# Left-over query tiles, 128-token blocks and a tighter pipeline in the first two batches of a fused attention and feed-forward kernel

## The chip, the cores and the metric

The kernel runs on one core of a Trainium2 chip. The metric is the device time of one execution in microseconds (us). The core has a matrix engine (TensorE, PE in the profile), whose weight loads are listed apart (PEld), a vector engine (VectorE, DVE), a scalar engine (ScalarE, ACT), a general engine (GpSimd, POOL) and a sync engine (SyncE, SP) that here only starts DMAs. Each engine has its own queue of instructions, and the kernel writes their order out by hand.

## The reference

Inputs are q, k and v of shape 8 x 8 x 576 x 64 (batches, heads, positions, head size) in float32, and the weights w_in (512 x 2048) and w_out (2048 x 512) in float64, which the kernel converts to float32 itself. What is computed:

```python
scores = scale * np.matmul(q, k.transpose(0, 1, 3, 2))
kth = np.partition(scores, -32, axis=-1)[..., -32:-31]
scores = np.where(scores >= kth, scores, -1000000000.0)
attn = np.exp(scores - np.max(scores, axis=-1, keepdims=True))
attn = attn / (np.sum(attn, axis=-1, keepdims=True) + 1e-09)
x = np.matmul(attn, v)        # -> tokens x 512
h = x @ w_in
out = (h * np.clip(h + 3.0, 0.0, 6.0) / 6.0) @ w_out
```

In words: attention in which each query keeps its 32 largest scores, and after it a feed-forward layer with a hard-swish between its two matrix products.

## The kernel before

**Tiles.** The 576 positions of a head are split into four tiles of 128 queries (qt 0 to 3) and 64 left-over queries (qt 4). Two heads make a Pair; two Pairs make a Duo, the unit of work. A batch has eight full duos (four tiles by two halves of the heads) and two left-over duos, ten in all, 80 in the kernel. In batches 0 to 6 a left-over duo stands after the two duos of tile 0 and another after those of tile 2; in batch 7 both stand after tile 0.

**Slots.** A duo is eight slots (loop `for i in range(8)`). In each slot `top` (L249, L253) makes one of four rounds that find the next eight largest of a row and strike them out: slots 0 to 3 for the first Pair, 4 to 7 for the second. A full duo has two rows per Pair and round, a left-over duo one. The scores of the next duo (L226, L229; L214, L216 for left-over ones) are issued in slot 1, in duo 0 in slot 3; ScalarE copies them from PSUM (L232, L235).

**Parts.** What follows the maxima is queued at fixed distances, in slots from the duo's start, separately for its two Pairs (tables `usual`, `early` for the first two duos and `soon` for the last two): `shift` (GpSimd, L262, L265), `exp` (ScalarE: two activations a row and the sum, L272, L277, L282), `inverse` (VectorE reciprocal, L286), `weights` (GpSimd: a multiply, L296, and a copy that splits words into 16-bit halves, L305), `flip` (a transposing DMA on SP, L311), `join` (puts the halves together, L317: ScalarE for the first Pair, GpSimd for the second) and `values` (the product with v on TensorE, L337, and ScalarE's copy to xT or xr, L344). In a full duo of the table `usual`, exp is at 4 and 8, values at 20.

**Feed-forward pieces.** When the values of a tile are complete, a block is put in the list `todo`: 128 tokens (16 pieces) in batches 0 and 7, 256 tokens (32 pieces) in batches 1 to 6, and 128 left-over rows of two batches together (xr, one buffer). A piece is 16 of the trace's matmuls of the first product (L361; 8 in a block of 256 tokens) or 4 of the second (L383). ScalarE takes the first product out of PSUM (L369, L371), GpSimd gates it (L375, L376). Per duo 6 to 9 pieces are issued (3 to 5 in a left-over duo), more when more are waiting (`left`). Before a new xT is begun, the pieces of the last block but one are all issued (`blocks[-2]`).

**Weight chunks.** w_in and w_out come in 32 chunks of 512 columns, one per slot. `convert` starts a DMA (L102); in a later slot ScalarE takes the absolute value (L108) and the low words (L111) and GpSimd clamps (L109); VectorE shifts and merges (L117, L118) and GpSimd adds (L122). With two chunks under way VectorE's and the add of the older are issued two slots after its clamp. All chunks are converted within the first four duos.

Of the kernel before, what the change touches and what calls it, by code (L numbers as in the profile page):

```python
# [29 lines left out]
def kernel(  # L30
# [9 lines left out]
    nc = tc.nc  # L40
    P = nc.NUM_PARTITIONS
    B, H, S, D = q.shape
    DM, FF = moe_w_in.shape
    J = S // P
# [51 lines left out]
    def convert(dst, src):  # L96

        st = kqpool.tile([P, 2 * WC], U32, tag="kq", name="st")
        nc.sync.dma_start(st[:], src)  # L102
        yield
        words = st[:].rearrange("p (n two) -> p n two", two=2)
        lo, hi = words[:, :, 0], words[:, :, 1]
        a = gpool.tile([P, WC], F32, tag="g", name="a")
        y = gpool.tile([P, WC], F32, tag="g", name="y")
        nc.scalar.activation(a[:], hi.bitcast(F32), AF.Abs)  # L108
        nc.gpsimd.tensor_scalar(a[:], a[:], HI_MOST, HI_LEAST, ALU.min, ALU.max)  # L109

        nc.scalar.activation(y[:], lo, AF.Copy, bias=2.0, scale=2.0**-51)  # L111
        yield

        au, yu = a[:].bitcast(U32), y[:].bitcast(U32)
        nc.vector.tensor_scalar(au, au, 3, None, ALU.logical_shift_left)  # L117
        nc.vector.scalar_tensor_tensor(  # L118
            out=yu, in0=hi, scalar=0x80000000, in1=yu,
            op0=ALU.bitwise_and, op1=ALU.bitwise_or,  # L120
        )
        nc.gpsimd.tensor_tensor(  # L122
            dst.bitcast(I32), a[:].bitcast(I32), y[:].bitcast(I32), ALU.add
        )
# [13 lines left out]
    class Pair:  # L138


        def __init__(self, b, hp):
            self.b, self.hp = b, hp
            self.vm, self.vr, self.kr = vms[hp], vrs[hp], krs[b % 2 * NHP + hp]
# [40 lines left out]
    class Duo:  # L184
# [4 lines left out]


        def __init__(self, pairs, qt):
            self.pairs, self.qt = pairs, qt
            self.rest = qt == J
            self.nt = 1 if self.rest else 2
            self.nb = J + 2 if self.rest else 2 * J + 1
            self.m, self.less = [None] * 2, [None] * 2
            self.e16, self.t16, self.eT = [None] * 2, [None] * 2, [None] * 2
# [115 lines left out]
        def join(self, u):  # L313

            eT = self.eT[u] = kqpool.tile([P, 2 * J + 1, P], F32, tag="kq", name="eT")
            copy = nc.gpsimd.tensor_copy if u else nc.scalar.copy
            copy(  # L317
                eT[:, 0 : self.nb, :]
                .rearrange("p c q -> p (c q)")
                .bitcast(U16)  # L320
                .rearrange("p (x h) -> p h x", h=2),
                self.t16[u][:, 0 : 2 * self.nb, :].rearrange("p (h c) q -> p h (c q)", h=2),
            )
# [77 lines left out]
    pairs = [[Pair(b, hp) for hp in range(NHP)] for b in range(B)]  # L401
    duos = []
    for b in range(B):
        halves = [pairs[b][0:2], pairs[b][2:4]]
        for qt in range(J):
            duos += [Duo(h, qt) for h in halves]

            if b == B - 1 and qt == 0:
                duos += [Duo(h, J) for h in halves]
            elif b < B - 1 and qt % 2 == 0:  # L410
                duos.append(Duo(halves[qt // 2], J))
    assert J == NHP == 4
    per_batch = 2 * J + 2
    ND = len(duos)
    todo = []
    blocks = []
    left = 0
# [2 lines left out]
    def piece(count=1):  # L420
        nonlocal left
        for _ in range(count):
            while todo:
                try:
                    gates.append(next(todo[0]))
                    left -= 1
                    break
                except StopIteration:
                    todo.pop(0)
            else:  # L430
                gates.append(None)
            if len(gates) > 2:
                gate = gates.pop(0)
                if gate:
                    gate()

    def queue(*block):
        nonlocal left
        todo.append(feed_forward(*block))
        if block[0] is not state.get("xr"):  # L440
            blocks.append(todo[-1])
        left += block[1] // 8

    state = {}

    def values(m):

        u = duos[m]
        b, qt, hp = u.pairs[0].b, u.qt, u.pairs[0].hp
        if u.rest:  # L450
            if b % 2 == 0 and hp == 0:
                state["xr"] = xrpool.tile([P, NHP, P], F32, tag="xr", name="xr")
            u.values(state["xr"][:, hp : hp + 2, (b % 2) * R : (b % 2 + 1) * R])
            if b % 2 == 1 and hp == 2:

                def rows(t0):
                    return [
                        (i * R, (i + 1) * R, out[(b - 1 + i) * S + JP : (b + i) * S, :])
                        for i in range(2)
                    ]  # L460

                queue(state["xr"], P, rows)
            return

        two = 0 < b < B - 1
        c0 = qt % 2 * P if two else 0
        if hp == 0 and c0 == 0:
            while len(blocks) > 1 and blocks[-2] in todo:
                piece()
            state["xT"] = xtpool.tile([P, NHP, 2 * P], F32, tag="xT", name="xT")  # L470
        u.values(state["xT"][:, hp : hp + 2, c0 : c0 + P])
        if hp == 2 and (not two or c0):

            def rows(t0):
                t = qt - c0 // P + t0 // P
                return [(0, P, out[b * S + t : b * S + JP : J, :])]

            queue(state["xT"], c0 + P, rows)

    chunks = list(weight_chunks())  # L480
    landing, converting = [], []

    def land(count=1):

        for _ in range(min(count, len(chunks))):
            c = convert(*chunks.pop(0))
            next(c)
            landing.append(c)

    def convert_step(depth=2):  # L490

        if len(converting) >= depth or not landing:
            for c in converting[:1]:
                next(c, None)
            del converting[:1]
        if landing:
            c = landing.pop(0)
            next(c)
            converting.append(c)
        land()  # L500

    def pair_at(m, first):
# [22 lines left out]
        shift0=3, exp0=4, inverse0=7, weights0=8, flip0=10, join0=13,  # L525
        shift1=7, exp1=8, inverse1=11, weights1=12, flip1=14, join1=17, values=20,
    )
    early = dict(
        shift0=3, exp0=3, inverse0=4, weights0=4, flip0=6, join0=8,
        shift1=7, exp1=7, inverse1=8, weights1=8, flip1=10, join1=12, values=13,  # L530
    )
    soon = dict(
        shift0=3, exp0=3, inverse0=5, weights0=5, flip0=7, join0=10,
        shift1=7, exp1=7, inverse1=9, weights1=9, flip1=11, join1=14, values=16,
    )
    queued = {}
    for m in range(ND):
        for part, at in (early if m < 2 else soon if m >= ND - 2 else usual).items():
            queued.setdefault(8 * m + at, []).append((m, part))

    def parts(slot):
        for m, part in sorted(queued.get(slot, []), key=lambda x: x[1][:-1] != "shift"):
            if part == "values":
                values(m)
            else:
                getattr(duos[m], part[:-1])(int(part[-1]))

    for m in range(ND + 3):
        u = duos[m] if m < ND else None

        level = (left >= 8) + (left >= 16) + (left >= 48)
        count = ((3, 4, 4, 5) if u and u.rest else (6, 7, 8, 9))[level]
        for i in range(8):
            if u:
                u.top(i // 4, i % 4)
            convert_step()
            if m == 0 and i == 0:
                first[3].load()
            if m == 0 and i in (1, 2):
                first[i + 1].transpose()  # L560
            if i == (3 if m == 0 else 1) and m + 1 < ND:
                duos[m + 1].scores()
            parts(8 * m + i)
            if m == 0 and i in (1, 4):
                for p in duos[i // 4].pairs:
                    p.load_values()
            if i == 0:
                p = pair_at(m, 4)
                if p:
                    p.load()  # L570
            if i == 3 and u and u.pairs[0].b and 1 <= m % per_batch <= 2:
                for p in duos[m - 1].pairs:
                    p.load_values()
            if i == 5:
                p = pair_at(m, 5)
                if p:
                    p.transpose()
            piece((i + 1) * count // 8 - i * count // 8)
# [36 lines left out]
```

## Time and profile before

| what | value |
|---|---|
| median of 3 runs | 1631.08 us (1630.5 to 1633.21) |
| span of the profiled execution | 1631.0 us |
| ScalarE, GpSimd busy | 1088.6 us (67%), 1140.9 us (70%) |
| mean granted TensorE clock | 0.951 |
| DMA, mean over the span | 88 GB/s |

The page divides the span into 40 slices of 40.8 us; a digit is the busy share of an engine in tenths. A row of the list of groups gives the line, engine and operation, the tiles written and read, the number of instructions, their busy time in us and the mean of one in ns, and then the idle time just before them with what ended it. In an answer about waits the columns are the waiting engine and line, what it waited for, the total in us, the number of waits and the longest. A row of the timeline gives the start in us, the duration in us, the engine, line and operation, the tiles, and in brackets the idle time before it and what ended it.

### The profile page before, as it was taken

To read this page: it belongs to the slowest core of one execution; us is meant where nothing else is said; L and a number is where in the kernel's file an instruction comes from. 1 tells how busy PE (TensorE), PEld (TensorE's weight loads), DVE (VectorE), ACT (ScalarE), POOL (GpSimd) and SP (SyncE) were. 2 spreads that over 40 slices of the span, in tenths; PEclk is the share of its full clock that TensorE was granted. 3 is DMA by queue.
4 is the path that set the end of the run, shared out by engine and by line. 5 is a ranking of instruction groups with operands and counts; after the bars stand their busy time and mean duration, and the time that the engine had idled before them with its cause. 6 is when DMAs were issued, how large, how long until landed. Compare 5 with 4: busy or idle time off the path is not lost.

```text
span 1631.0 us, 25648 instructions
## 1 busy us (share of the span) xinstructions
PE 1466.9 (90%) x8736; PEld 979.2 (60%) x8736; DVE 1470.0 (90%) x3105; ACT 1088.6 (67%) x1863; POOL 1140.9 (70%) x1266
## 2 busy tenths in 40 slices
PE   5147699848999999899999999898999999899999
PEld 2134467627567584756567584656577584657775
DVE  5999999999999989999999889999999889999500
ACT  5566677667777676767767676767767676757521
POOL 3787577757787776867787776867787775867741
PEclk9568799979999999999999999999999999999999
DMA  8553434444444434454344424454354424333410
GB/s 231 156 171 64 101 63 89 97 95 83 71 98 99 94 56 92 86 109 85 65 104 89 94 56 92 88 107 84 65 105 89 94 56 94 80 60 72 66 22 13
DMA packets 450307, 144.29 MB, mean 88 GB/s; under 512 B 433280, under 2 KB 441472, under 8 KB 450176
## 3 DMA queue, kind: packets, MB, share of 16 engines
q1 hardware_dynamic: 450176, 142.65, 42.3%
q8 instruction: 69, 1.13, 0.3%
q14 instruction: 62, 0.51, 0.1%
HBM read 45.09 MB, written 9.44 MB: 33 GB/s over the span
## 4 chain that ended last, share of the span: by engine, by line
DVE 48%; PE 43%; ACT 3%; POOL 3%; SPq 1%; issue 1%; DMA 0%; POOLq 0%; ACTq 0%
DVE m L249 25%; DVE wk L253 20%; PE acc L383 16%; PE h L361 15%; PE pv L337 5%; PE big L226 3%; DVE y L118 1%; POOL eT L317 1%; PE big L229 1%; ACT sc L277 1%; DVE a L117 1%; SPq L150 1%; POOL sc L296 1%; PE big L214 1%; SPq L154 1%
## 5 line engine op out<-in xcount | busy, mean ns | idle before, releaser
L249 DVE MAX8 m<-wk 128x8 f32<-128x576 f32 x864 | 614.5, 748 | 3.1
L383 PE MATMUL acc<-w_out,g 128*128 128x512 f32 x1152 | 517.9, 600 | 5.1 <-POOL g L376 5.1
L361 PE MATMUL h<-xT,w_in 128*128 128x256 f32 (+1 forms) x2560 | 472.5, 343 | 0.0
L361 PEld LDWEIGHTS h<-xT,w_in 128*128 128x128 f32 x2560 | 410.0, 194 | 48.4 <-issue 10.3
L253 DVE MATCH_REPLACE8 wk<-m,wk 128x576 f32<-128x576 f32 x576 | 423.8, 742 | 0.0
L383 PEld LDWEIGHTS acc<-w_out,g 128*128 128x128 f32 x1152 | 213.5, 191 | 244.6 <-issue 234.6
L305 POOL COPY e<-sc 128x2304 uint16<-128x2304 uint16 (+1 forms) x192 | 322.0, 1687 | 10.1
L337 PE MATMUL pv<-eT,vm 128*64 128x128 f32 (+1 forms) x2560 | 169.1, 278 | 119.3 <-POOL eT L317 84.8
L272 ACT ACTIVATE sc<-sc,m 128x576 f32<-128x576 f32 x288 | 209.7, 773 | 47.5 <-DVE m L249 47.1
L337 PEld LDWEIGHTS pv<-eT,vm 128*64 128x64 f32 x2560 | 138.2, 144 | 161.7 <-POOL eT L317 89.6
L277 ACT ACTIVATE sc<-sc,shift 128x576 f32<-128x576 f32 x288 | 219.8, 766 | 21.5 <-POOL shift L265 18.7
L296 POOL TENSOR_SCALAR sc<-sc,den 128x576 f32<-128x576 f32 x288 | 213.0, 750 | 27.6 <-DVE den L286 27.1
L262 POOL TENSOR_TENSOR shift<-m 128x2 f32<-128x2 f32 (+1 forms) x160 | 32.1, 201 | 269.7 <-DVE den L286 266.8
L317 POOL COPY eT<-t 128x2304 uint16<-128x2304 uint16 (+1 forms) x80 | 208.5, 2606 | 5.7 <-DMA t<-e 4.6
L253 DVE MATCH_REPLACE8 wk<-m,sc 128x576 f32<-128x576 f32 x288 | 211.9, 742 | 0.0
L317 ACT COPY eT<-t 128x2304 uint16<-128x2304 uint16 (+1 forms) x80 | 208.9, 2611 | 0.0
L249 DVE MAX8 m<-sc 128x8 f32<-128x576 f32 x288 | 202.9, 741 | 0.9 <-ACT sc L235 0.9
L376 POOL TENSOR_TENSOR g<-g,hs 128x512 f32<-128x512 f32 x144 | 183.7, 1276 | 12.0
L344 ACT COPY xT<-pv 128x256 f32<-128x256 f32 x64 | 23.8, 372 | 232.8 <-PE pv L337 232.8
L375 POOL TENSOR_SCALAR g<-g 128x512 f32<-128x512 f32 x144 | 88.6, 615 | 95.3 <-ACT g L369 85.4
L226 PE MATMUL big<-kq 64*128 64x512 f32 x512 | 133.0, 638 | 10.3 <-ACT kr L182 10.3
L369 ACT ACTIVATE g<-h,three 128x512 f32<-128x512 f32 x144 | 98.4, 684 | 62.3 <-PE h L361 59.8
(47 smaller groups left out, 1210.4 us busy)
## 6 DMA issues: line engine op xcount, KB each, us to landing
landed<-in_k_dram SPq DMA_DIRECT2D x64, 128.0 KB, 3.0
landed<-in_q_dram SPq DMA_DIRECT2D x64, 128.0 KB, 2.9
st<-in_moe_w_in_dram SPq DMA_DIRECT2D x16, 512.0 KB, 5.0
vm<-in_v_dram SPq DMA_DIRECT2D x64, 128.0 KB, 2.3
st<-in_moe_w_out_dram SPq DMA_DIRECT2D x16, 512.0 KB, 3.8
out_dram<-o SPq DMA_DIRECT2D x32, 256.0 KB, 2.4
t<-e SPq DMA_TRANSPOSE x160, 4.6
landed<-in_k_dram SPq DMA_DIRECT2D x32, 32.0 KB, 2.6
```

Source lines behind the costliest of these rows:

```text
L226: nc.tensor.matmul(banks[:, 2 * i + hh, :], pr.qT[d, qs], pr.kT[d, :])
L249: nc.vector.max(self.m[u][:, t, 8 * r : 8 * r + 8], self.cur[t])
L253: nc.vector.match_replace(wk, self.m[u][:, t, 8 * r : 8 * r + 8], self.cur[t], LOWEST)
L272: nc.scalar.activation(row, row, AF.Prelu, bias=m[:, t, TOP_K - 1 : TOP_K], scale=-1.0, alpha=FLAT)
L277: nc.scalar.activation(row, row, AF.Exp, bias=self.less[u][:, t : t + 1], scale=-scale / FLAT, accum_out=self.den[:, u, t : t + 1],)
L296: nc.gpsimd.tensor_scalar(row, row, self.den[:, u, t : t + 1], 1.0, ALU.mult, ALU.mult)
L305: nc.gpsimd.tensor_copy(halves[:, :, to : to + c1 - c0], words)
L317: copy(eT[:, 0 : self.nb, :] .rearrange("p c q -> p (c q)") .bitcast(U16) .rearrange("p (x h) -> p h x", h=2), self.t16[u][:, 0 : 2 * self ...
L337: nc.tensor.matmul(pv[hh * D : (hh + 1) * D, u * w : (u + 1) * w], pr.vm[:, hh, c, :] if c < J else pr.vr[:, hh, :], rhs, start=(c == 0), ...
L361: nc.tensor.matmul(h[:, (f - f0) * nt : (f - f0 + 1) * nt], w_in[:, i, f * P : (f + 1) * P], xT[:, i, 0:nt], start=(i == 0), stop=(i == NH ...
L376: nc.gpsimd.tensor_tensor(g[:], g[:], hs[:], ALU.mult)
L383: nc.tensor.matmul(acc[:], gs[f // nf][:, c0 : c0 + P], w_out[:, f, :], start=(f == 0), stop=(f == NFC - 1),)
```

## The change

- In batches 0 and 1 both left-over duos stand at the end, after tile 3. Batches 2 to 7 keep their order.
- Batch 1's blocks have 128 tokens instead of 256.
- In the first two duos flip, join and values come earlier: flips at 5 and 9 instead of 6 and 10, joins at 7 and 11 instead of 8 and 12, values at 11 instead of 13; the second join goes from GpSimd to ScalarE.
- Duo 1's scores are issued in slot 4 of duo 0 instead of slot 3.
- The conversion has four parts instead of three: the add has a slot of its own, and in every slot each chunk under way takes a step, so that VectorE's part is one slot after the clamp and the add one slot after that.
- In the first four duos the parts of a slot other than inverse and weights are issued before the slot's conversion steps, inverse and weights after the scores as before.
- Before the first left-over values of an even batch, all waiting pieces up to the block that uses xr are issued.

```diff
+        yield
         nc.gpsimd.tensor_tensor(
             dst.bitcast(I32), a[:].bitcast(I32), y[:].bitcast(I32), ALU.add
...
-            copy = nc.gpsimd.tensor_copy if u else nc.scalar.copy
+            copy = nc.gpsimd.tensor_copy if u and not self.early else nc.scalar.copy
...
-            if b == B - 1 and qt == 0:
+            if qt == (0 if b == B - 1 else J - 1) and not 1 < b < B - 1:
                 duos += [Duo(h, J) for h in halves]
-            elif b < B - 1 and qt % 2 == 0:
+            elif 1 < b < B - 1 and qt % 2 == 0:
                 duos.append(Duo(halves[qt // 2], J))
...
+    for u in duos[:2]:
+        u.early = True
...
             if b % 2 == 0 and hp == 0:
+                while state.get("rest") in todo:
+                    piece()
...
-        two = 0 < b < B - 1
+        two = 1 < b < B - 1
...
-    def convert_step(depth=2):
-        if len(converting) >= depth or not landing:
-            for c in converting[:1]:
-                next(c, None)
-            del converting[:1]
+    def convert_step():
+        begun = list(converting)
+        for c in begun:
+            if next(c, "done") == "done":
+                converting.remove(c)
...
-        shift0=3, exp0=3, inverse0=4, weights0=4, flip0=6, join0=8,
-        shift1=7, exp1=7, inverse1=8, weights1=8, flip1=10, join1=12, values=13,
+        shift0=3, exp0=3, inverse0=4, weights0=4, flip0=5, join0=7,
+        shift1=7, exp1=7, inverse1=8, weights1=8, flip1=9, join1=11, values=11,
...
+            if m < 4:
+                parts(8 * m + i, False)
             convert_step()
...
-            if i == (3 if m == 0 else 1) and m + 1 < ND:
+            if i == (4 if m == 0 else 1) and m + 1 < ND:
                 duos[m + 1].scores()
-            parts(8 * m + i)
+            if m < 4:
+                parts(8 * m + i, True)
+            else:
+                parts(8 * m + i)
```

More of the change, by code (lines that the diff above doesn't have):

```diff
@@ L191, in __init__ @@
         def __init__(self, pairs, qt):
-            self.pairs, self.qt = pairs, qt
+            self.pairs, self.qt, self.early = pairs, qt, False
             self.rest = qt == J
@@ L462, in values @@
                 queue(state["xr"], P, rows)
+                state["rest"] = todo[-1]
             return
-        two = 0 < b < B - 1
+        two = 1 < b < B - 1
         c0 = qt % 2 * P if two else 0
@@ L539, with parts @@
             queued.setdefault(8 * m + at, []).append((m, part))
-    def parts(slot):
+    def parts(slot, late=None):
         for m, part in sorted(queued.get(slot, []), key=lambda x: x[1][:-1] != "shift"):
+            if late is not None and (part[:-1] in ("inverse", "weights")) != late:
+                continue
             if part == "values":
```

## The prediction

> **What bounds the kernel now.** I read the page's slices first, then the waits of VectorE, then stretches of the timeline around each wait. The engines' shares alone mislead: TensorE and VectorE are both 90% busy.
>
> ```profile
> PE 1466.9 (90%) x8736; PEld 979.2 (60%) x8736; DVE 1470.0 (90%) x3105; ACT 1088.6 (67%) x1863; POOL 1140.9 (70%) x1266
> PE   5147699848999999899999999898999999899999
> DVE  5999999999999989999999889999999889999500
> ...
> L249 DVE MAX8 m<-wk 128x8 f32<-128x576 f32 x864 | 614.5, 748 | 3.1
> ```
>
> The DVE row is full from the second slice to the third from the end, and TensorE alone runs in the last two and a half. TensorE's holes (slices 2 to 5 and the 4 in slice 9) lie beside a full VectorE. The waits of VectorE, in total and up to 140 us:
>
> ```profile
> DVE den L286 <- ACT den L282: 48.9, 18, 10.0
> DVE a L117 <- POOL a L109: 10.8, 1, 10.8
> ...
> DVE den L286 <- ACT den L282: 11.2, 4, 7.9
> ```
>
> So VectorE loses 48.9 us to one kind of wait, the reciprocal waiting for ScalarE's exponentials; 11.2 of it before 140 us. By counting MAX8 in the timeline I gave each wait its duo. A full duo takes 19.40 us of VectorE, a left-over one 11.34, a converted chunk 0.93 to 3. The waits over 3 us are 7.93 in duo 0, 5.93 in duo 27, 10.02 in 47, 9.96 in 67, 4.72 after the last search. The last search ends near 1533 and the last reciprocal at 1537.6; the 93 us after that are the pieces that program order puts there.
>
> The wait of duo 0 (timeline):
>
> ```profile
> 37.48 1.45 ACT L272 ACTIVATE sc<-sc,m 128x576 f32<-128x576 f32 x2
> ...
> 40.47 0.20 ACT L282 ACTIVATE den<-den 128x2 f32<-128x2 f32 x1
> ...
> 40.70 0.17 DVE L286 RECIPROCAL den<-den 128x2 f32<-128x2 f32 x1 [7.93 <-ACT den L282]
> ```
>
> The maxima were ready at 27.6; ScalarE came to the exponentials at 37.48 because the copies of duo 1's scores, which TensorE delivered at 35.4, stand before them in its queue. The wait of duo 27:
>
> ```profile
> 559.63 10.46 PE L383 MATMUL acc<-w_out,g 128*128 128x512 f32 x24
> 569.93 1.89 PE L361 MATMUL h<-xT,w_in 128*128 128x256 f32 x8
> 571.75 1.09 PE L337 MATMUL pv<-eT,vm 128*64 128x128 f32 x16
> ...
> 574.20 0.37 ACT L344 COPY xT<-pv 128x256 f32<-128x256 f32 x1 [3.47 <-PE pv L337]
> ...
> 576.48 0.16 DVE L286 RECIPROCAL den<-den 128x1 f32<-128x1 f32 x1 [5.93 <-ACT den L282]
> ```
>
> Pieces drained ahead of values hold TensorE, ScalarE's copy of pv waits for it, the exponentials queue behind the copy, VectorE waits.
>
> **What the Trainium skill says.** "PSUM — Partial Sum Buffer", section Engine vs sequencer instructions: ScalarE, VectorE and GpSimd queues are strict FIFO, and matmuls keep program order. Both stretches agree. "SBUF — State Buffer", section Who interferes with whom: the read and write ports that VectorE shares with GpSimd are an exclusive lock; the second to issue blocks until the first is done. The trace agrees:
>
> ```profile
> 59.12 2.17 POOL L305 COPY e<-sc 128x2304 uint16<-128x2304 uint16 x1
> ...
> 59.26 2.58 DVE L118 SCALAR_TENSOR_TENSOR y<-st,y 128x512 uint32<-128x512 uint32 x1
> ```
>
> The same instruction takes 0.68 beside an idle GpSimd and ends here 0.55 after the copy. MAX8 shows no such delay.
>
> **The change, part by part.** Sums are against the profiled span of 1631.0; the runs are 1630.5 to 1633.2, so I add the difference to their median, 1631.08.
>
> *TensorE's work, the tail, the matmul shapes: 0.* A 128-token block costs 14.3 (128 matmuls at L361) + 13.9 (32 at L383); a 256-token block twice that. I walked the queue of pieces by hand: from duo 47 on both programs issue the same pieces in the same slots, so the 93 us tail stays. Batch 1's earlier blocks fill TensorE's hole at 340 to 380 (20.2 busy of 40), but VectorE is 40.00 of 40.00 there, which hides the gain completely.
>
> *First slots (part A).* Now a chunk is absolute value and clamp in slot s, VectorE's two instructions in s+2. After: clamp in s, VectorE in s+1, the add in s+2. Chunk 1 thus stands ahead of the first search. ScalarE has its absolute value at 13.36 (after the score copy), the clamp ends near 14.7, GpSimd's add of chunk 0 (1.27) takes the lock, so chunk 1 ends near 17.1 and the search starts there instead of at 13.51. Chunk 3 still can't end before 26.2 (its clamp waits for scores until 23.7), now one search (2.77) behind. In slot 3 the exponentials (3.5) stand ahead of duo 1's scores, which go to slot 4: denominators near 34.8 instead of 40.67. But chunk 6's clamp is behind them (36.2), VectorE needs it at 35.2 and then loses the lock to an add. I get 39.0 for the reciprocal's end with chunk 6 converted, against 40.87 with chunk 5: a gain of 1.9 + 0.93 = 2.8 at slot 4.
>
> *Slots 5 to 24.* Wherever the round-4 maximum comes (each fourth slot), the exponentials, and now the join, stand on ScalarE before the chunk's absolute value, and VectorE wants its clamp after only 0.93 + 2.77 = 3.7. Slot 8: join 2.7, exponentials 3.5, absolute 0.6, clamp 0.6: 2.1 wait and 1.3 lock, and the gain is -0.4. Slots 11 and 12: join1, the matmuls of values (2.4 at the low clock of this stage), the 0.37 copy, duo 1's exponentials 3.5 and then chunk 14: e is copied by 61.3 and lands as t near 65.9 (median 4.6), the clamp ends at 76.5, VectorE there at 71.3; with the lock 6.5 lost, minus what the old schedule lost: -5.6. Slot 16: -4.8 (before has 2.00 there). Slot 20 (join1 and values of duo 1 in slot 19): 3.0 lost. At the start of duo 3 I have 126.9 against 114.56 + 8.06 (full for left-over duo) + 1.3 (one chunk more) = 123.9. **A: 3.0 lost**, between 5 gained (ScalarE less late by a join) and 9 lost (GpSimd, 77 to 88% busy there, late too). u=1's copies leave GpSimd (2 x 2.75), which the wait for the clamp doesn't repay. Flips stand before the landings on SP: a landing held behind a flip loses up to 3 us, against a lead of three slots (about 12): nothing.
>
> *Left-over duos in pairs (part B).* A lone one costs 11.34 to 11.79. The only pair now, in batch 7, has waits of 0.48 and 1.82, since two in a row take 22.7 of VectorE while TensorE needs 12.4 to 14 for each (scores 2.5, four pieces 7.0, values 2.9, a transpose 1.1). Pairs in batches 0 and 1: 1.5 each. **B: 3 lost**, from 0 to 5.
>
> *The drain of left-over rows (part C).* The block of rest rows is queued at slot 8x19+20, duo 21. Batch 2's first rest values come at 8x22+20, duo 24, slot 4. Left at the start of duo 24 are 13 pieces; three go out, so 10 are drained, where before none were. From the scores of duo 25: 2.5 + 3x1.75 + 10x1.75 + values 1.3 = 26.5, copy 0.3, exponentials 3.5: 30.3. VectorE gets from that slot to its reciprocal in 17.0. The wait is 13.3 less TensorE's lead over VectorE, 3.6 at duo 28's scores in the trace and 0 to 7 elsewhere; with 4, 9.3. Drawn for duo 27 the same sum gives 5.9 (measured 5.93). Then the queue is empty for a duo and a half, so at duo 27 nothing is drained: 5.9 gained. At duo 47 five pieces are drained instead of seven: 2x1.75 = 3.5 gained. **C: 0.1 lost** (+4 to -4).
>
> Sum: 3.0 + 3 + 0.1 = 6.1 slower, 1631.1 + 6.1 = 1637.
>
> **Rivals.**
> 1. *Faster: the waits of the first duos go and none takes their place*, because the clamps come in time: A is -11.2 (the four waits before 140 us), with B and C as forecast 1631.1 - 11.2 + 3.1 = 1623. For it: ScalarE is at 10 to 15 of 20 busy up to 140 us. Against: FIFO order behind join and exponentials. It decides if the three clamps of slots 7, 11 and 15 come within 3.7 us of their maxima. Chance 0.22.
> 2. *TensorE's hole is worth its length:* 20 us off, 1611. Against: the same pieces from duo 47, and VectorE full. Counted inside rival 1, 0.03 of it.
> 3. *It cancels:* A about -3, the rest as forecast: 1631. Chance 0.20.
> 4. *GpSimd becomes the bound of the conversion:* weights and copy (4.2), add, clamp and gates (1.9) make it a slot late in six further places of duos 1 to 3 at 2 us: A is 15 lost, 1648 or more. It decides from 8 us of GpSimd work between two conversions. Chance 0.13.
>
> **How the numbers follow.** The forecast (1634 to 1645) has 0.45. What a measurement tells from no change is 0.2%, 3.3 us. Faster: 0.22 from rivals 1 and 2. Same: rival 3 and the near edge of the forecast, 0.22. Slower: 0.56. The range leaves the far half of rival 1 and the far half of rival 4 out: 1621 to 1648.
>
> **What would show it.** First MAX8 near 17 instead of 13.51; no wait of 7.9 at the first reciprocal; VectorE's waits at L117 for GpSimd's clamp in slots 8, 12, 16 and 20, the one near 71 to 77 the largest; a wait at a reciprocal in duo 24 of about 9 us behind ten drained pieces, none in duo 27, 6 to 7 in duo 47, 10 still in duo 67; the tail after the last reciprocal 93 us; TensorE's slice 9 filled and a new hole at 520 to 560. I am wrong if the L117 waits sum to under 5 us, or if TensorE leads by over 8 at duo 24.

## The result and the profile after

The changed kernel takes 1640.47 us (median of 4 runs, 1640.33 to 1641.05), the kernel before 1631.5 us (4 runs): a ratio of 1.0055, 95% interval 1.0037 to 1.0072, so 6 to 12 us slower. The forecast was 1637 us, with a range of 1621 to 1648. The profiled spans are 1638.5 and 1631.0. They differ by 7.5 us and the medians by 9.0, because the profiled execution of the kernel before was one of 1632.77 us, 1.3 above the median; the sums below are against the spans.

The page of the changed kernel, engines' totals and slices (one slice is now 41.0 us):

```profile
PE 1475.4 (90%) x8992; PEld 992.8 (61%) x8992; DVE 1473.8 (90%) x3105; ACT 1092.9 (67%) x1865; POOL 1135.5 (69%) x1264
PE   5245889889999699898999999899999999899999
DVE  6899999999998899999999989999999989999600
...
L250 DVE MAX8 m<-wk 128x8 f32<-128x576 f32 x864 | 614.7, 748 | 3.3
```

TensorE's 4 in slice 9 is now an 8: the early hole is filled. From 335 to 380 us TensorE is busy for 40.35 us, before for 21.70. A new 6 stands in slice 14. VectorE is as full as before, and the time is longer all the same. (In the changed kernel the lines from L122 on have numbers one higher.) VectorE's waits over the whole span, then from 140 to 560 us, and last from 140 to 560 us in the kernel before:

```profile
DVE den L287 <- ACT den L283: 43.2, 15, 10.8
DVE a L117 <- POOL a L109: 20.9, 8, 10.1
...
DVE den L287 <- ACT den L283: 16.4, 5, 10.8
...
DVE den L286 <- ACT den L282: 0.3, 1, 0.3
```

All 20.9 us of L117 lie before 140 us, and there no reciprocal waits any more (11.2 us before). In its place the chunks' L117 waits for GpSimd's clamp: 10.1 for the first chunk, which waited 10.8 before, and 10.8 in sum in seven new waits. From 140 to 560 us, where the kernel before had one wait of 0.34, there are now 16.4.

The largest of the seven new waits is in slot 12 (slots are counted from the start of duo 0, so this is slot 4 of duo 1). Timelines of ScalarE, GpSimd and VectorE:

```profile
64.50 2.76 ACT L318 COPY eT<-t 128x2304 uint16<-128x2304 uint16 x1 [5.78 <-DMA t<-e]
69.78 0.37 ACT L345 COPY xT<-pv 128x256 f32<-128x256 f32 x1 [2.53 <-PE pv L338]
70.05 1.44 ACT L273 ACTIVATE sc<-sc,m 128x576 f32<-128x576 f32 x2
...
73.15 0.65 ACT L108 ACTIVATE a<-st 128x512 f32<-128x512 f32 x1
...
73.88 0.61 POOL L109 TENSOR_SCALAR a<-a 128x512 f32<-128x512 f32 x1 [4.54 <-ACT a L108]
74.46 1.27 POOL L123 TENSOR_TENSOR w_in<-a,y 128x512 int32<-128x512 int32 x1
...
74.53 1.49 DVE L117 TENSOR_SCALAR a<-a 128x512 uint32<-128x512 uint32 x1 [4.01 <-POOL a L109]
```

ScalarE goes from join to the copy of pv (waiting for TensorE between them) to the exponentials and only then to the chunk's absolute value. VectorE waits 4.01, and when the clamp is done GpSimd's next instruction, the add, starts 0.07 before L117 and has the shared ports. L117 takes 1.49 where it takes 0.40 beside an idle GpSimd.

Such blocking lies inside an instruction's duration and stands in no list of waits. L117 and L118 up to 160 us, before and then after:

```profile
L118 DVE SCALAR_TENSOR_TENSOR y<-st,y 128x512 uint32<-128x512 uint32 x32 | 33.5, 1046 | 0.0
L117 DVE TENSOR_SCALAR a<-a 128x512 uint32<-128x512 uint32 x32 | 23.3, 727 | 10.8 <-POOL a L109 10.8
...
L118 DVE SCALAR_TENSOR_TENSOR y<-st,y 128x512 uint32<-128x512 uint32 x32 | 32.7, 1021 | 0.0
L117 DVE TENSOR_SCALAR a<-a 128x512 uint32<-128x512 uint32 x32 | 27.1, 846 | 20.9 <-POOL a L109 20.9
```

Together the two lines take 59.8 us for 56.8 before, while VectorE's waits in this stage fell from 22.9 us (10.8, 11.2 and 0.9 at a first search) to 20.9. So the first stage did not lose by waiting longer, but by blocking.

The largest wait of the second kind, at the reciprocal, is in duo 24. Timelines of TensorE, ScalarE and VectorE's wait in the chip's order:

```profile
511.10 9.10 PE L362 MATMUL h<-xr,w_in 128*128 128x128 f32 x80
520.03 13.90 PE L384 MATMUL acc<-w_out,g 128*128 128x512 f32 x32
533.86 0.69 PE L338 MATMUL pv<-eT,vm 128*64 128x64 f32 x16
...
535.29 0.27 ACT L345 COPY xr<-pv 128x128 f32<-128x128 f32 x1 [0.73 <-PE pv L338]
535.46 1.44 ACT L273 ACTIVATE sc<-sc,m 128x576 f32<-128x576 f32 x2
...
538.44 0.20 ACT L283 ACTIVATE den<-den 128x2 f32<-128x2 f32 x1
...
538.68 0.17 DVE L287 RECIPROCAL den<-den 128x2 f32<-128x2 f32 x1 [10.77 <-ACT den L283]
```

TensorE runs 13 pieces, the ten drained ones among them, without a gap (23 us of L362 and L384) and then the left-over values; ScalarE's last job before was at 521.5, and the exponentials of duo 24 stand behind the copy to xr. VectorE waits 10.77 for them.

By counting MAX8 again, the 7.5 us between the spans:

| stretch | before | after | difference |
|---|---|---|---|
| start of duo 4 (before: plus 8.06 for a full duo in a left-over one's place) | 144.71 + 8.06 | 154.73 | +2.0 |
| pairs: duos 9 and 19 at 14.35 for 11.34, less 0.45 in duo 12 of before | | | +5.6 |
| duo 24 | 19.40 | 30.26 | +10.9 |
| duo 27 | 17.39 | 11.34 | -6.0 |
| duo 47 | 21.46 | 17.90 | -3.6 |
| all else (single duos, each 0.6 or less) | | | -1.4 |

### The profile page after: what moved, and what is told of

The parts are those of the page before. It is cut to its first block, busy times and chain, and to the rows that moved or that the text cites. A ratio compares the mean times of both kernels' runs of the same rounds, so it can differ in the third digit from the quotient of the medians.

```text
span 1638.5 us, 26151 instructions
## 1 busy us (share of the span) xinstructions
PE 1475.4 (90%) x8992; PEld 992.8 (61%) x8992; DVE 1473.8 (90%) x3105; ACT 1092.9 (67%) x1865; POOL 1135.5 (69%) x1264
## 4 chain that ended last, share of the span: by engine, by line
DVE 52%; PE 34%; POOL 6%; ACT 4%; issue 2%; DMA 1%; SPq 1%; POOLq 0%; ACTq 0%
DVE m L250 28%; DVE wk L254 23%; PE acc L384 13%; PE h L362 12%; PE pv L338 4%; PE big L227 2%; POOL eT L318 2%; POOL e L306 1%; ACT eT L318 1%; POOL sc L297 1%; DMA t<-e 1%; ACT sc L278 1%; PE big L230 1%; DVE y L118 1%; ACT sc L273 1%
## 5 line engine op out<-in xcount | busy, mean ns | idle before, releaser
L384 PE MATMUL acc<-w_out,g 128*128 128x512 f32 x1152 | 520.6, 602 | 13.2 <-POOL g L377 13.2
L362 PE MATMUL h<-xT,w_in 128*128 128x128 f32 (+1 forms) x2816 | 473.5, 327 | 0.0
L362 PEld LDWEIGHTS h<-xT,w_in 128*128 128x128 f32 x2816 | 419.7, 194 | 42.1 <-issue 9.6
L384 PEld LDWEIGHTS acc<-w_out,g 128*128 128x128 f32 x1152 | 214.6, 193 | 254.0 <-issue 235.2
L306 POOL COPY e<-sc 128x2304 uint16<-128x2304 uint16 (+1 forms) x192 | 320.0, 1677 | 10.1
L338 PE MATMUL pv<-eT,vm 128*64 128x128 f32 (+1 forms) x2560 | 172.5, 281 | 114.1 <-POOL eT L318 58.3
L263 POOL TENSOR_TENSOR shift<-m 128x2 f32<-128x2 f32 (+1 forms) x160 | 35.5, 222 | 302.8 <-DVE den L287 283.5
L318 ACT COPY eT<-t 128x2304 uint16<-128x2304 uint16 (+1 forms) x82 | 214.5, 2615 | 25.1 <-DMA t<-e 25.1
L318 POOL COPY eT<-t 128x2304 uint16<-128x2304 uint16 (+1 forms) x78 | 202.6, 2597 | 4.0 <-DMA t<-e 3.2
```

The lines of the kernel that those rows point to most:

```text
L306: nc.gpsimd.tensor_copy(halves[:, :, to : to + c1 - c0], words)
L318: copy(eT[:, 0 : self.nb, :] .rearrange("p c q -> p (c q)") .bitcast(U16) .rearrange("p (x h) -> p h x", h=2), self.t16[u][:, 0 : 2 * self ...
L338: nc.tensor.matmul(pv[hh * D : (hh + 1) * D, u * w : (u + 1) * w], pr.vm[:, hh, c, :] if c < J else pr.vr[:, hh, :], rhs, start=(c == 0), ...
L362: nc.tensor.matmul(h[:, (f - f0) * nt : (f - f0 + 1) * nt], w_in[:, i, f * P : (f + 1) * P], xT[:, i, 0:nt], start=(i == 0), stop=(i == NH ...
L384: nc.tensor.matmul(acc[:], gs[f // nf][:, c0 : c0 + P], w_out[:, f, :], start=(f == 0), stop=(f == NFC - 1),)
```

## The experiments

Theory: VectorE sets the time, and it loses or gains what ScalarE's exponentials and the chunks' clamps lose or gain in their queues. Rival: TensorE has the same pieces to do anyway, so a wait taken away in one place comes back in another. Ratios are to the kernel before, run beside each set of experiments. Its medians in the three sets (1631.5, 1631.6 and 1631.9) agree within 0.4 us, so the runs can also be compared with the changed kernel, which was measured in the first set.

**The old order of the duos in the changed kernel.**

```diff
-            if qt == (0 if b == B - 1 else J - 1) and not 1 < b < B - 1:
+            if b == B - 1 and qt == 0:
                 duos += [Duo(h, J) for h in halves]
-            elif 1 < b < B - 1 and qt % 2 == 0:
+            elif b < B - 1 and qt % 2 == 0:
```

> The changed kernel with one part undone: left-over duos of batches 0 and 1 stand after tiles 0 and 2 again. Theory (two new places where exponentials queue behind TensorE: the drain at duo 24, 10.8 us, and the pairs at duos 9 and 19, 2.8 us each): these waits go, nothing is drained before duo 47, so some 15 us less than the changed kernel, near 1625 us. Rival (TensorE has that work to do anyway and the wait only moves to the next full queue): no more than 5 us less, 1635 us or above.

Measured: 1628.96 us, ratio 0.9983 (0.9976 to 0.9991), so 11.5 less than the changed kernel, where 15 were expected. VectorE's waits from 140 to 560 us:

```profile
DVE den L287 <- ACT den L283: 1.7, 2, 1.3
```

16.4 has become 1.7: the 15 us were there, and the wait did not move. The other 3.4 were lost in the first duos: a left-over duo among the chunks has short slots, so the clamp's lead is shorter, and L117 waits 2.34, 0.33 and 3.62 there, for 1.08 and 0.92 in the changed kernel. Duo 4 starts at 150.05, where the changed kernel, corrected for the duo's length, has 146.67. Putting the left-over duos last therefore helped the conversion by 3.4 us and cost 15 elsewhere.

**A second buffer for the left-over rows.**

```diff
-    xrpool = pool("xr", 1)
+    xrpool = pool("xr", 2)
...
-                while state.get("rest") in todo:
-                    piece()
```

> The changed kernel with two buffers for the left-over rows and without the drain ahead of them. Theory: the reciprocal's wait of 10.8 us in duo 24 goes and comes back nowhere, since duo 27 drains nothing and duo 47 still five pieces (6.4 us): 1629 to 1630 us. Rival (the drained pieces are only delayed and hold ScalarE later): the sum of VectorE's waits falls by less than 5 us, 1636 us or above.

Measured: 1629.58 us, ratio 0.9988 (0.9981 to 0.9994): 10.9 less than the changed kernel for a wait of 10.77. The waits from 440 to 1530 us, in the changed kernel and then in this one:

```profile
DVE den L287 <- ACT den L283: 32.9, 10, 10.8
...
DVE den L287 <- ACT den L283: 22.3, 9, 9.8
```

Nothing came back later. The wait belonged to one buffer of 2 KB per partition, and to the drain that is needed when there is only one.

**Chunks in three parts.** The extra `yield` and the new `convert_step` of the change are taken out.

> The changed kernel with the chunks converted in three parts again (VectorE's part and the add two slots after the clamp). Theory (the one-slot lead is what VectorE waits for): first search near 13.5 instead of 16.47, no waits at L117 after it, reciprocals of the first duos wait 1 to 3 us for their exponentials instead; 6 to 10 us less than the changed kernel, 1631 to 1634 us. Rival (exponentials and join on ScalarE set the pace whatever the lead): the reciprocal takes over the whole wait, 1638 us or above.

Measured: 1634.14 us, ratio 1.0016 (1.0009 to 1.0022): 6.3 less than the changed kernel. First search at 13.37; up to 140 us:

```profile
DVE a L117 <- POOL a L109: 10.7, 3, 10.0
DVE den L286 <- ACT den L282: 9.6, 4, 4.8
```

The clamp's waits go and the reciprocals wait in their place, 4.81 in slot 12, more than the 1 to 3 that were expected. So a lead of two slots doesn't remove the crowding on ScalarE in slots 7 to 12: VectorE's waits in this stage are even 0.9 longer in sum (21.8 for 20.9). Duo 4 starts 6.1 earlier all the same, since L117 and L118 take 7 us less over the 32 chunks; their means fall from 846 to 673 ns and from 1021 to 976. The expected time came, but not for the theory's reason: what the two-slot lead saves is blocking, and the waiting only passes to the reciprocals, as the rival had it.

**Duo 1's scores in slot 4, in the kernel before.**

```diff
-            if i == (3 if m == 0 else 1) and m + 1 < ND:
+            if i == (4 if m == 0 else 1) and m + 1 < ND:
```

> The kernel before with one edit: duo 1's scores in slot 4 of duo 0 instead of slot 3. Theory: the exponentials stand ahead of the score copies, the reciprocal's wait of 7.93 us goes to under 1, and everything after it comes as much earlier: 1623 to 1625 us. Rival (duo 1's first search then waits for scores, or the gain is lost behind TensorE later): under 2 us gained, 1629 us or above.

Measured: 1625.38 us, ratio 0.9962 (0.9947 to 0.9977). The wait of 7.93 is 2.01, since VectorE comes to it at 32.3 and the denominators are done at 34.3; so 6 us were gained of the 8. The wait that is left is longer than the expected 1, but the gain is not lost again later.

**The first two duos' parts where they were, in the changed kernel.** The table `early` and the engine of the second join as before.

> The changed kernel with the first two duos' parts where they were (flips 6 and 10, joins 8 and 12, values 13, second join on GpSimd). Theory (join1 and values in slot 11 stand ahead of the exponentials and of chunk 14's absolute value, and join0 ahead of exp1 in slot 7): the wait of 4.01 us at L117 in slot 12 falls to about 1, that in slot 8 to under 0.5, 3 to 6 us less than the changed kernel, 1635 to 1637 us. Rival (the exponentials alone make the clamp late): those waits stay and the time is within 2 us of the changed kernel.

Measured: 1637.96 us, ratio 1.0035 (1.0021 to 1.0049): 2.5 less than the changed kernel. The waits up to 140 us:

```profile
DVE a L117 <- POOL a L109: 16.0, 7, 10.4
```

In slot 12 the wait falls from 4.01 to 0.49, in slot 8 from 1.24 to 0.77. The theory's mechanism holds in slot 12; in slot 8 most of the wait stays, which fits the rival, that the exponentials alone keep the clamp late. The gain of 2.5 lies between the theory's 3 to 6 and the rival's 2, and the intervals of the two ratios overlap. In the trace duo 4 starts 2.4 earlier: the waits are 4.5 shorter up to there, but L117 and L118 take 2.1 longer, and in slot 12 L117 alone takes 2.97 instead of 1.49. Half of what was gained by waiting less was lost again by blocking.

**Values after exp, in the changed kernel.** Since three of the waits had one form, the order of two parts in a slot was turned round.

```diff
-        for m, part in sorted(queued.get(slot, []), key=lambda x: x[1][:-1] != "shift"):
+        for m, part in sorted(queued.get(slot, []),
+                              key=lambda x: (x[1] == "values", x[1][:-1] != "shift")):
```

> The changed kernel with one edit: in a slot, values (TensorE's product and ScalarE's copy of it) is issued after exp, not before. Theory (VectorE waits because exponentials stand behind that copy in ScalarE's queue): the waits of duos 9, 19, 24, 47, 67, 73 and 76 (2.1 + 2.1 + 10.8 + 6.4 + 9.8 + 1.7 + 2.7 = 35.6 us) fall to a few us in sum; the time falls by what TensorE can follow, whose idle time from 440 to 1545 us is 46 us: 1606 to 1620 us. Rival (TensorE is late itself and VectorE then waits for scores instead): less than 5 us gained, 1635 us or above.

Measured: 1616.41 us, ratio 0.9903 (0.9889 to 0.9918), 24 less than the changed kernel. From 440 to 1530 us:

```profile
DVE den L287 <- ACT den L283: 19.2, 7, 4.7
```

The first Pair's reciprocal no longer waits, but the second's now does, half a duo later: 4.40 in duo 25, 1.25 in duo 48, 4.66 in duo 68, where the second exponentials queue behind the delayed copy. So part of the wait moved after all, and more than the expected few us in sum is left. These 19.2 include the last reciprocal's 4.7, which in the changed kernel falls after 1530 us, so the sum fell from 37.6 to 19.2; duo 4 starts 2.5 earlier (slot 12 waits 1.33 for 4.01), and the two pairs save 3.8.

**Scores in slot 4 and values after exp, in the kernel before.**

> The kernel before with two edits: duo 1's scores in slot 4 of duo 0, and values after exp within a slot. Theory: against scores in slot 4 alone (1625.4 us) the waits of duos 27, 47, 67, 73 and 76 (5.9 + 9.9 + 9.8 + 2.2 + 2.7 = 30.5 us) nearly go; TensorE has only 25 us of idle time from 560 to 1531 us and becomes the bound: 1601 to 1612 us. Rival (the wait moves to scores or to the copies of them): 1620 us or above.

Measured: 1608.95 us, ratio 0.9858 (0.9843 to 0.9873). The waits of duos 27, 47 and 67 (5.94, 9.94 and 9.75 with the scores in slot 4 alone) have become 1.23, 5.42 and 5.40, each in the next duo. That is more than "nearly go", and whether TensorE has become the bound is not shown: from 560 to 1514 us it is busy for 939.7 us of 954 and VectorE for 928.3.

**The same with 128-token blocks in batch 1.**

```diff
-        two = 0 < b < B - 1
+        two = 1 < b < B - 1
```

> The two edits of the run before and blocks of 128 tokens in batch 1, one part of the change. Theory (TensorE is the bound once VectorE's waits are gone, so its hole of some 20 us at 340 to 380 us is now worth something): 3 to 15 us less than without the blocks. Rival (program order is the same again from duo 47 on, and VectorE still sets the time there): within 2 us of the run without the blocks.

Measured: 1604.11 us, ratio 0.9828 (0.9814 to 0.9843), 27.7 us below the kernel before and the best of all. The gain of 4.8 is in the theory's range, but the trace does not show the theory's reason. TensorE idles more from 420 to 560 us than without the blocks (131.24 busy of 140 for 139.64), and VectorE keeps waits of its own over the whole span:

```profile
DVE den L286 <- ACT den L282: 21.0, 10, 5.4
```

The gain is at two drains: duo 28's wait of 1.23 is gone and duo 48's is 1.23 instead of 5.42, since the earlier blocks leave no pieces to drain in duo 27 and five instead of seven in duo 47. Duo 68, where both drain seven, keeps its 5.4. The blocks are worth what they spare the drains, not the length of TensorE's hole.

## Why the prediction was right, point by point

- *VectorE sets the time and the tail stays.* Right: the tail after the last reciprocal is 93.2 in both, though TensorE's hole at 340 to 380 was filled.
- *Part A, 3.0 lost.* Measured 2.0, but put together differently, so that the size is near by luck. The reciprocal of slot 4 ended at 37.8 (forecast 39.0): the first search began at 16.47, not 17.1, and chunk 6 waited 0.79. The waits in slots 8 and 12 were taken too large: 1.24 for a forecast of 2.1, and 4.01 of wait and 1.1 of lock for a forecast of 6.5. In slot 12 the join began at 64.50, where t was expected only at 65.9, and with it the exponentials and the clamp came earlier (clamp done at 74.49 for 76.5). At the start of duo 3 the changed kernel was still 0.7 ahead (123.23 against 123.9). What was missing is duo 3: it took 31.50 for six chunks (2.0 a chunk) where the kernel before had 30.15 for seven (1.5), with no wait there. L118 beside GpSimd's copy took 2.58 and beside a gate 1.75. I had taken 1.3 a chunk. The 8.06 for the longer duo 2 was low too: from the starts of its instructions I estimate 9.2 there, because among chunks the searches of a left-over duo took 10.3 us and not the 11.3 that they take alone.
- *Part B, 3 lost.* The mechanism was right, the size was not: 5.6, beyond the end of 5 that I gave. Each pair lost 3.0, since beside the wait behind the copy to xT (2.05) the reciprocal of the duo ahead waits 0.75, for which batch 7's pair shows 0.23. But 1.5 was low from the start: the two waits that I read in batch 7's pair, 0.48 and 1.82, already make 2.3. A lone left-over duo cost up to 11.93 in the trace before (duo 42), and not 11.79.
- *Part C, 0.1 lost.* Measured +1.3: duo 24 waited 10.77 for a forecast of 9.3, because TensorE's lead was 2.6 (scores at 508.64, VectorE's first search of that slot at 511.26) and not 4. With 2.6 the sum gives 10.7. Duos 27 and 47 came out at 6.0 and 3.6 gained for 5.9 and 3.5.
- *The sum.* The forecast was 6.1 lost, and 7.5 are lost between the spans, 9.0 between the medians. A came out 1.0 lower than forecast, B 2.6 and C 1.2 higher, and all else gave 1.4 back. The direction and the mechanisms were foreseen; that the sum is so near is in part luck.
- *Chances.* The clamps came too late for rival 1, the filled hole gained nothing for rival 2, and part A lost where rival 3 had it gain. Of rival 4 duo 3 showed a little: VectorE blocked by GpSimd without a wait, some 3 us (six chunks at 2.0 for 1.5).

What the runs leave open: whether the 1.4 us in small waits are one thing, and how much of duo 3's lock time comes from the gates and how much from the order of GpSimd's adds. Nor was it tried alone to issue the other parts before a slot's conversion steps, which the change does in the first four duos, or to use the changed kernel with batch 1's blocks of 256.

## What to carry to other kernels

Where a hand-written order puts a copy that waits for a slow engine ahead of work that the bounding engine needs, the copy's wait becomes the bounding engine's: look in each queue for what stands behind the waiting instruction, and issue the urgent work first. Filling another engine's hole is worth nothing by itself if the bounding engine is full beside it. A pipeline with one more step can have a shorter lead at the step that matters, so count slots between producer and consumer, not steps. And where two engines share ports, compare the durations of their instructions too: a list of waits does not show what one loses to the other.

## What the runs showed of the hardware that was not expected

- In all seven new waits of L117 for GpSimd's clamp, GpSimd's next operation, an add, started first (in slot 12 at 74.46 against 74.53), and L117 then took 1.48 to 1.49 us instead of 0.40. Each of these waits cost about 1.1 us more than the wait itself. The first chunk's wait of 10.1, with no add behind the clamp, cost nothing more: L117 took 0.43.
- Blocking grew where waiting shrank: up to duo 4 VectorE's waits fell from 22.9 to 20.9 us, while L117 and L118 together rose from 56.8 to 59.8. In duo 3 no wait is listed, but L117 and L118 took 13.0 us for six chunks, where 0.41 and 0.68 each would make 6.5.
